# Sigmoid attention and mixture of depths: moving one pair's transposes and products between gaps of the attention steps

## The chip, the cores and the metric

The kernel runs on one core of a Trainium2 chip. Its time is device microseconds of one execution; before the change the median of 3 runs is 457.12 us (456.84 to 457.91). The profiled execution took 455.25 us, of which the profile shows a span of 453.4 us, at a mean granted TensorE clock of 0.996. All times within the execution are microseconds from the start of that span.

## The reference

```python
# attention: q, k, v are (8, 12, 448, 64), float32
scores = scale * q @ k^T - log(448)
attn   = 1 / (1 + exp(-scores))
x      = (attn @ v), heads joined -> (8, 448, 768)

# mixture of depths, w1 (768, 1024), w2 (1024, 768), capacity 128
for b in range(8):
    scores = x[b] @ w_gate
    top    = indices of the 128 largest scores
    xe     = x[b, top]
    h      = maximum(xe @ w1, 0)
    ye     = h @ w2
    out[b]      = x[b]
    out[b, top] = xe + sigmoid(scores[top])[:, None] * ye
```

All is float32. So a sequence's attention has to be complete before its 128 rows can be chosen, and only chosen rows go through the two matrices.

## The kernel before

**Steps and units.** Attention runs in 12 steps (`s` = 0 to 11). A step takes two groups of four heads, and three groups make a sequence, so a sequence is finished every one and a half steps. A step has 7 units (`n` = 0 to 6). `unit(s, n)` makes scores for both halves of the heads into two PSUM tiles `psc` (pool `ps_sc`, two buffers, so every unit uses both) with 32 recorded matmuls (L305), and ScalarE turns each tile into `attn_...` with one sigmoid of 128x896 (L313). After each unit comes `gap(s, n)`. Gaps 0 to 2 and 6 hold the products of the attention with `v` (`values`, L353): those of part 1 to 3 of step `s - 1` in gaps 0 to 2, part 0 of step `s` in gap 6. `take` (L368) turns the finished output into `x_b` in SBUF on VectorE.

**The choice of rows.** `gates` (L376, L379) multiplies `x_b` with the gate weights and sums, on VectorE; `gate` finishes the 448 scores of a sequence and writes them to DRAM (L404), `spread` reads them back broadcast over the partitions (`rep`, L416), `ranking` counts for each token how many are larger (L424, L427) and makes the selection mask `hot` (L439). `choose` is a small product of TensorE with the mask (L467, or L463 for some sequences), `fetch` turns its result into indices (L474, L477) and gathers the 128 rows `xe` from `out` (L488).

**The two matrices.** Sequences are taken in pairs `p`, so each product's weights are used for both. `turn_rows(b)`, written `("t", b)` in the table, transposes the rows of a sequence with six products with a unit matrix (L509); for the even sequence of a pair ScalarE copies the result to `rows_t` (L512), for the odd one ScalarE and VectorE copy half each (L514, L515), and VectorE makes three differences (L521) and, once product 2 has read its row, a last one (L531). Each of the two matrix products for a pair is done in the form with seven products of quarter matrices in place of eight, numbered 1 to 7. In the table `(m, p, key)` is product `key` of matrix `m` for pair `p`. `first` is 12 matmuls in the code, 24 records in the profile (L548), and its sums over `hidden` are on VectorE (L561) with rectifiers on ScalarE (L564, or the copy L567 for product 1); `second` is 4 in the code, 8 records (L613), and `second_sums` adds the result to `xe` on VectorE (L624), one operation for each quarter of `QUARTERS[key]`; the last one starts the scatter of the rows to `out` (L633). `hidden_sum` (L595, L599) makes four further sums of the hidden rows.

**What sets the order.** The schedule is written out by hand: each engine executes its instructions in the order in which the Python emits them, and waits are put in where one engine needs another. `WORK` says which transposes and products stand in gaps 3 to 5 of each step; they fill TensorE while ScalarE works on the sigmoids. Pairs 0 and 1 are done within the steps. Pair 2 (sequences 4 and 5) is begun in step 11 and done in `rest()`, the end part, followed by pair 3. In `rest()` the last sequence's scores, ranking and choice run on VectorE and the DMA queues while TensorE goes through pair 2.

**PSUM.** `banks(which)` hands out tiles of two banks: `psc` (two buffers) and two further ones, `o0` and `o1`. `"o"` alternates between these two, `"any"` alternates between `psc` and `o`. Within the steps, the transposes, products and `choose` take `"o"`, so a third user in a gap waits until the first one's tile has been read; `gap(s, 2)` sets the alternation back, so that the first in gap 3 has `o0`. `values(s, 0)` takes both.

**Weights.** Some quarter matrices stay in SBUF (`w1_sb`, `w2_sb`); the sums are kept in DRAM and lent (L208) into space of the attention: `LENT[11]` brings those of products 6, 7 and 5 of the first matrix into slots `d00` to `d02` as soon as step 10's attention output has been computed.

Of the kernel before, what the change touches and what calls it, by code (L numbers as in the profile page):

```python
# [17 lines left out]
def kernel(  # L18
# [475 lines left out]
    def bank(where):  # L494
        return banks(where)[:, 0]
# [42 lines left out]
    def first(p, key, where="o", ps=None):  # L538
        n = CAP
        x = pairs[p]["x"][:, ROWS1[key]]  # L540
        if key == 1:
            t = moe.tile([P, 7 * FH * P], F32, name="hidden")
            pairs[p]["h"] = t.rearrange("p (m k n) -> p m k n", m=7, k=FH)
        w = weight(1, key, p)
        ps = (bank(where) if ps is None else ps).rearrange("p (k n) -> p k n", n=P)
        for f in range(FH):
            for t in range(KH):
                nc.tensor.matmul(ps[:, f, :n], w((t * FH + f) * P, P), x[:, t, :n],  # L548
                                 start=(t == 0), stop=(t == KH - 1))
        if key == 2:  # L550
            pairs[p]["second"] = True
            last_row(p)
        return p, key, ps
# [77 lines left out]
    def scatter(b):  # L631
# [16 lines left out]
        (8, 3): [("t", 3), (1, 1, 1)], (8, 4): [(1, 1, 2), (1, 1, 6)],  # L648
        (8, 5): [(1, 1, 7), (1, 1, 4)],
        (9, 3): [(2, 1, 1), (2, 1, 2)], (9, 4): [(1, 1, 5)], (9, 5): [(1, 1, 3), (2, 1, 4)],  # L650
        (10, 3): [(2, 1, 3)], (10, 4): [(2, 1, 5), (2, 1, 6)], (10, 5): [(2, 1, 7)],
        (11, 3): [("t", 4)], (11, 4): [("t", 5), (1, 2, 1)], (11, 5): [(1, 2, 2)],
    }

    LENT = {5: [(1, 6), (1, 7), (1, 5)], 6: [(1, 3), (2, 4), (2, 5)], 7: [(2, 6), (2, 7)],
# [3 lines left out]
    def begin(item, where="o"):  # L659

        m, p, key = item
        return (first if m == 1 else second)(p, key, where)
# [87 lines left out]
    def rest():  # L750
# [4 lines left out]
        p, b = NP - 2, B - 1  # L755
        for key, slot in (((2, 6), "d10"), ((2, 7), "d11")):
            lend(*key, slot)
        shared = banks("any")
        chosen = choose(b - 1, shared[:, 1])
        work = [((1, p, 6), first(p, 6, ps=shared[:, 0])),  # L760
                ((1, p, 7), begin((1, p, 7), "any"))]
        gates(2 * NS - 1)
        fetch(*chosen)

# [3 lines left out]
        store(b, (2, 3))  # L768
        for item, args in work:
            finish(item, args)  # L770
        for key in (4, 5):
            do((1, p, key), "any")
        first_sums(*begin((1, p, 3), "any"), sums_too=(5, 6))
        work = {key: begin((2, p, key), "any") for key in (2, 1, 4)}
        ranking(b)
        tile5 = banks("any")
        work[5] = second(p, 5, ps=tile5[:, 0])
        chosen = choose(b, tile5[:, 1])
        second_sums(*work[2])
        hidden_sum(p, 7)  # L780
        work[6] = begin((2, p, 6), "any")
        fetch(*chosen)
        second_sums(*work[1])
        hidden_sum(p, 3)
        work[7] = begin((2, p, 7), "any")
        for key in (4, 5, 6, 7):
# [95 lines left out]
```

## Time and profile before

| engine | busy, us | share of the span |
|---|---|---|
| TensorE (PE) | 442.0 | 97% |
| TensorE weight loads (PEld) | 267.0 | 59% |
| VectorE (DVE) | 303.8 | 67% |
| ScalarE (ACT) | 181.8 | 40% |
| GpSimd (POOL) | 32.5 | 7% |

Busy shares of these engines by stage, and what the DMA engines did:

| window, us | what runs | PE | DVE | ACT | DMA share | GB/s |
|---|---|---|---|---|---|---|
| 320 to 340 | end of step 10 | 20.00 | 11.12 | 7.79 | 0.53 | 147 |
| 340 to 360 | step 11 | 19.41 | 11.37 | 11.38 | 0.65 | 164 |
| 360 to 380 | step 11, start of the end part | 18.84 | 11.61 | 3.28 | 0.95 | 211 |
| 380 to 400 | pair 2 | 20.00 | 18.45 | 1.23 | 0.77 | 171 |
| 400 to 420 | pair 2, pair 3 | 20.00 | 11.88 | 2.71 | 0.18 | 60 |
| 420 to 440 | pair 3 | 20.00 | 11.94 | 1.26 | 0.00 | 1 |

A row of a timeline has the start, the length, the engine, the line, the operation, its output and inputs, its shape, and the count of instructions merged into it; in brackets stands how long the engine was idle before it and whose work ended the wait. Matmuls overlap, so the length of a merged row is somewhat longer than the distance to the next row's start. A row also counts as busy while a later instruction in it waits.

### The profile page before, as it was taken

Reading aid. Unit: us, or ns where it says so; the run is one execution under the profiler, and the core shown is the slowest. Engines: PE = TensorE matmul, PEld = TensorE weight load, DVE = VectorE, ACT = ScalarE, POOL = GpSimd, SP = SyncE. Lnnn points to the kernel's source line nnn. Section 1 sums busy time; section 2 is a strip of 40 time slices with the busy share of each in tenths; the row PEclk is TensorE's granted clock in tenths of the full one; section 3 lists DMA queues with packets and bytes.
Section 4 is the critical chain, followed back from the end, with each engine's and each line's share of the span. In section 5 each row is a group of like instructions: output and inputs, shape, how many; then the busy total and the mean of one; then the engine's idle time right before and its main releaser. Section 6 shows DMA issues by size and latency. Waiting matters only on the chain.

```text
span 453.4 us, 14452 instructions
## 1 busy us (share of the span) xinstructions
PE 442.0 (97%) x6398; PEld 267.0 (59%) x6398; DVE 303.8 (67%) x663; ACT 181.8 (40%) x237; POOL 32.5 (7%) x55
## 2 busy tenths in 40 slices
PE   8999999999999999999999999999999989999994
PEld 3474745565745845554445855654454639769952
DVE  4308679993844797887634697897742849994472
ACT  3856464555555254335444345334345520101100
POOL 7000000010000100000100000010010000001001
PEclk9999999999999999999999999999999999999998
DMA  8898898999866995995566883994833999811001
GB/s 279 214 329 193 329 342 187 267 205 319 175 201 220 139 234 192 170 233 186 117 235 174 132 222 142 193 196 159 241 106 101 259 189 267 147 37 71 1 0 69
DMA packets 128334, 84.67 MB, mean 187 GB/s; under 512 B 97600, under 2 KB 112064, under 8 KB 128272
## 3 DMA queue, kind: packets, MB, share of 16 engines
q1 hardware_dynamic: 126288, 75.84, 65.1%
q0 software_dynamic: 1984, 7.91, 5.7%
q8 instruction: 50, 0.82, 0.8%
q14 instruction: 12, 0.10, 0.1%
HBM read 63.28 MB, written 20.46 MB: 185 GB/s over the span
## 4 chain that ended last, share of the span: by engine, by line
PE 93%; DVE 3%; issue 1%; ACT 1%; DMA 1%; POOLq 0%; DVEq 0%; ACTq 0%
PE o L353 28%; PE psc L305 27%; PE o L548 13%; PE o L613 12%; PE psc L548 4%; PE psc L613 3%; PE o L305 3%; PE o L818 1%; PE o L326 1%; DVE x_b L368 1%; DMA out_dram<-xe,idx 1%; ACT attn_u L313 1%; DVE gate_p L379 1%; DVE scr L376 1%; PE o L467 0%
## 5 line engine op out<-in xcount | busy, mean ns | idle before, releaser
L305 PE MATMUL psc<-qT,kT 32*64 32x448 f32 x2496 | 148.2, 540 | 0.9 <-ACT attn_u L313 0.9
L313 ACT ACTIVATE attn_u<-psc,bias_s 128x896 f32<-128x896 f32 x86 | 81.9, 1004 | 84.4 <-PE psc L305 84.3
L353 PE MATMUL o<-attn_d,raw_v 32*64 32x448 f32 x960 | 104.5, 535 | 0.4 <-ACT o L356 0.4
L353 PE MATMUL o<-attn_u,raw_v 32*64 32x448 f32 x960 | 102.2, 535 | 0.8 <-ACT o L356 0.8
L305 PEld LDWEIGHTS psc<-qT,kT 32*64 32x64 f32 x2496 | 60.2, 131 | 59.1 <-issue 40.3
L313 ACT ACTIVATE attn_d<-psc,bias_s 128x896 f32<-128x896 f32 x70 | 66.7, 1003 | 46.5 <-PE psc L305 46.4
L368 DVE STREAM_TRANSPOSE x_b<-o 128x448 f32<-128x448 f32 x48 | 26.9, 618 | 66.6 <-PE o L353 59.3
L353 PEld LDWEIGHTS o<-attn_u,raw_v 32*64 32x64 f32 x960 | 41.2, 132 | 24.9 <-issue 19.9
L353 PEld LDWEIGHTS o<-attn_d,raw_v 32*64 32x64 f32 x960 | 40.4, 132 | 19.9 <-issue 17.3
L548 PEld LDWEIGHTS o<-rows_t,w_sb 128*128 128x128 f32 x264 | 30.4, 192 | 4.5 <-issue 1.4
L548 PEld LDWEIGHTS o<-rows_t,attn_d 128*128 128x128 f32 x264 | 30.3, 192 | 3.9 <-DVE scr L376 1.4
L548 PE MATMUL o<-rows_t,w_sb 128*128 128x128 f32 x264 | 31.9, 278 | 0.4 <-DVE rows_t L515 0.3
L548 PE MATMUL o<-rows_t,attn_d 128*128 128x128 f32 x264 | 31.6, 277 | 0.3 <-DVE rows_t L521 0.3
L379 DVE TENSOR_REDUCE gate_p<-scr 128x14 f32<-128x448 f32 x48 | 29.8, 622 | 1.7
L376 DVE TENSOR_TENSOR scr<-x_b,wg_b 128x448 f32<-128x448 f32 x48 | 29.6, 616 | 1.0
L624 DVE SCALAR_TENSOR_TENSOR xe<-o,gate,xe 128x384 f32<-128x384 f32 x37 | 21.1, 611 | 13.4 <-PE o L613 13.3
L280 DVE STREAM_TRANSPOSE kT<-raw_k 128x384 f32<-128x384 f32 x46 | 23.5, 548 | 6.9 <-PE psc L305 3.6
L613 PE MATMUL o<-attn_d,hidden 128*128 128x384 f32 x80 | 27.7, 494 | 0.0
L564 ACT ACTIVATE hidden<-hidden 128x512 f32<-128x512 f32 x12 | 7.5, 630 | 48.1 <-DVE hidden L561 48.1
L424 DVE TENSOR_SCALAR_CACHE_REDUCE scr<-rep,who 128x448 f32<-128x448 f32 (+1 forms) x32 | 21.5, 671 | 7.2 <-DMA rep<-scores 6.2
L613 PE MATMUL o<-w_sb,hidden 128*128 128x384 f32 x72 | 24.7, 491 | 0.0
L561 DVE TENSOR_TENSOR hidden<-o,hidden 128x512 f32<-128x512 f32 x24 | 16.0, 686 | 12.0 <-PE o L548 11.8
(117 smaller groups left out, 478.3 us busy)
## 6 DMA issues: line engine op xcount, KB each, us to landing
attn_d<-sum SPq DMA_DIRECT2D x42, 384.0 KB
out_dram<-x_b SPq DMA_DIRECT2D x32, 336.0 KB
raw_k<-in_k_dram SPq DMA_DIRECT2D x23, 448.0 KB
raw_q<-in_q_dram SPq DMA_DIRECT2D x23, 448.0 KB
raw_v<-in_v_dram SPq DMA_DIRECT2D x40, 192.0 KB
w_sb<-in_moe_w_dram SPq DMA_DIRECT2D x6, 768.0 KB
sum<-hidden SPq DMA_DIRECT2D x6, 768.0 KB
rep<-scores POOLq DMA_DIRECT2D x7, 224.0 KB, 5.3
```

The lines of the kernel that those rows point to most:

```text
L280: nc.vector.transpose(kT[i][:, e, :HK], sk[:, e, :HK].rearrange("p (m c) d -> p c m d", c=NF))
L305: nc.tensor.matmul(psc[h // 2][y * Dh:(y + 1) * Dh, h % 2, :S], kT[2 * s + x][d, e, r:r + 2, :].rearrange("d r t -> d (r t)"), qT[2 * s + ...
L313: nc.scalar.activation(a, psc[pr][:, :, :S], AF.Sigmoid, bias=bias_s, scale=QK_SCALE)
L353: nc.tensor.matmul(o[x][j * Dh:(j + 1) * Dh, pr, :S], w, a[rows, j, :], start=(n == 0 and c == 0), stop=(n == 3 and c == NF - 1))
L368: nc.vector.transpose(x_tiles[b][:, :, 2 * g + pr, :], outs[s][x][:, pr, :S].rearrange("p (r t) -> p r t", t=TT))
L376: nc.vector.tensor_tensor(out=tmp, in0=x_tiles[b][:, :, hp, :], in1=wg_b[:, hp:hp + 1, :].to_broadcast([P, TB, TT]), op=ALU.mult)
L379: nc.vector.tensor_reduce(out=gate_parts[b][:, :, hp], in_=tmp, axis=AX.X, op=ALU.add)
L424: nc.vector.tensor_scalar(out=junk[:n], in0=rep[:n], scalar1=own, scalar2=0.0, op0=ALU.is_gt, op1=ALU.add, accum_out=above[:n, c:c + 1])
L548: nc.tensor.matmul(ps[:, f, :n], w((t * FH + f) * P, P), x[:, t, :n], start=(t == 0), stop=(t == KH - 1))
L561: nc.vector.tensor_tensor(out=dst, in0=a, in1=b, op=ALU.add)
L613: nc.tensor.matmul(ps[:n, :DH], h[:, t, :n], w(t * DH, DH), start=(t == 0), stop=(t == FH - 1))
L624: nc.vector.scalar_tensor_tensor(out=xe[:n, cols], in0=ps[:n, :DH], scalar=st[b]["gate"][:n, 0:1], in1=xe[:n, cols], op0=ALU.mult, op1=ALU ...
```

## The change

Three edits belong together.

- In the table, the transposes of sequence 4 move from gap 3 of step 11 to the end of gap 5 of step 10. The three gaps of step 11 are filled anew: product 1 of pair 2 in gap 3, the transposes of sequence 5 and product 2 in gap 4, product 6 in gap 5. Before, they held the transposes of sequence 4; those of sequence 5 and product 1; product 2. So every gap is to have a product, and one product more of pair 2 is done within step 11.
- In `rest()`, product 6 is therefore gone from the end part. Products 7 and 4 of the first matrix are now those that are issued ahead of the last gate work, then 5 and 3.
- Of the second matrix, products 1 and 2 change places, both where they are issued and where their sums are taken.

```diff
-        (10, 3): [(2, 1, 3)], (10, 4): [(2, 1, 5), (2, 1, 6)], (10, 5): [(2, 1, 7)],
-        (11, 3): [("t", 4)], (11, 4): [("t", 5), (1, 2, 1)], (11, 5): [(1, 2, 2)],
+        (10, 3): [(2, 1, 3)], (10, 4): [(2, 1, 5), (2, 1, 6)], (10, 5): [(2, 1, 7), ("t", 4)],
+        (11, 3): [(1, 2, 1)], (11, 4): [("t", 5), (1, 2, 2)], (11, 5): [(1, 2, 6)],
...
-        work = [((1, p, 6), first(p, 6, ps=shared[:, 0])),
-                ((1, p, 7), begin((1, p, 7), "any"))]
+        work = [((1, p, 7), first(p, 7, ps=shared[:, 0])),
+                ((1, p, 4), begin((1, p, 4), "any"))]
...
-        for key in (4, 5):
-            do((1, p, key), "any")
+        do((1, p, 5), "any")
         first_sums(*begin((1, p, 3), "any"), sums_too=(5, 6))
-        work = {key: begin((2, p, key), "any") for key in (2, 1, 4)}
+        work = {key: begin((2, p, key), "any") for key in (1, 2, 4)}
         ranking(b)
         tile5 = banks("any")
         work[5] = second(p, 5, ps=tile5[:, 0])
         chosen = choose(b, tile5[:, 1])
-        second_sums(*work[2])
+        second_sums(*work[1])
         hidden_sum(p, 7)
         work[6] = begin((2, p, 6), "any")
         fetch(*chosen)
-        second_sums(*work[1])
+        second_sums(*work[2])
         hidden_sum(p, 3)
```

The number and the kind of the instructions of every engine stay as they were; only their order and the banks of some products differ.

## The prediction

> **What bounds the kernel now.** I read the page's busy table first, then the chain of waits, then TensorE's own timeline where the change falls, then VectorE's and ScalarE's beside it. Steps are named as in the code: (11, 3) is the gap after unit 3 of step 11.
>
> ```profile
> PE 442.0 (97%) x6398; PEld 267.0 (59%) x6398; DVE 303.8 (67%) x663; ACT 181.8 (40%) x237; POOL 32.5 (7%) x55
> PE 93%; DVE 3%; issue 1%; ACT 1%; DMA 1%; POOLq 0%; DVEq 0%; ACTq 0%
> ```
>
> TensorE is the bound, with 11 us of its 453.4 us span without work, and 7% of the chain lies on other engines. The edit keeps every product, so it can pay only by closing idle time of TensorE, and it costs whatever idle it opens. A "busy" matmul row also stretches over a wait in its middle, so I compare start times. TensorE at the end of step 10 and in step 11:
>
> ```profile
> 327.97 2.85 PE L613 MATMUL o<-attn_d,hidden 128*128 128x384 f32 x8
> 330.65 0.50 PE L463 MATMUL o<-ones,sums 128*128 128x1 f32 x4
> 331.08 1.76 PE L305 MATMUL psc<-qT,kT 32*64 32x448 f32 x32
> ...
> 349.37 0.85 PE L509 MATMUL o<-iden,xe 128*128 128x128 f32 x6
> 350.55 2.65 PE L305 MATMUL psc<-qT,kT 32*64 32x448 f32 x32 [0.33 <-ACT attn_u L313]
> 353.12 0.87 PE L509 MATMUL o<-iden,xe 128*128 128x128 f32 x6
> ...
> 358.63 2.94 PE L548 MATMUL o<-rows_t,w_sb 128*128 128x128 f32 x24 [0.26 <-DVE rows_t L515]
> ```
>
> An unhindered unit takes 1.70 us from start to next start, a set of turned rows (six transposes) 0.7, a product 2.7 (first matrix) or 2.6 (second). After the first six transposes of step 11, unit 4 should begin at 350.03 and be over at 351.72. It is over at 353.12: the 0.7 us of work in gap 3 is too short to cover ScalarE emptying the score banks of unit 3 (two sigmoids, 349.48 to 351.39). Lost: 1.40 us. The rest of gaps 3 to 5 holds another 0.68 us, half of it the 0.26 wait in the last line. So step 11 offers about 2.08 us.
>
> In the end part TensorE runs without a gap from 375.65, the selection product of sequence 6 (this moment is T below), to its last matmul. But VectorE is barely ahead there:
>
> ```profile
> 392.94 0.68 DVE L424 TENSOR_SCALAR_CACHE_REDUCE scr<-rep,who 128x448 f32<-128x448 f32 x1 [0.37 <-DMA rep<-scores]
> ...
> 398.93 0.69 DVE L439 TENSOR_TENSOR hot<-slots,place_s 128x512 f32<-128x512 f32 x1
> 399.54 0.61 DVE L624 SCALAR_TENSOR_TENSOR xe<-o,gate,xe 128x384 f32<-128x384 f32 x1
> ```
>
> Sequence 7's selection mask `hot` is ready at 399.62, T + 23.97. TensorE asks for it at 400.37, T + 24.72. Slack 0.75 us, and the ranking ahead of it began when the broadcast of the scores landed. That is a chain of fixed length from T (attention output, gates, scores out, scores back, ranking), and TensorE's work beside it is what the edit shortens.
>
> [...] the 0.26 us wait of a product on L515 lies behind 0.62 us gate operations on VectorE that have nothing to do with it. [...] I use that as the lower bound for the scores' write, which took from 386.03 (end of its issue) to 389.93, when the read back could be issued: 3.9 us.
>
> **The change part by part.** All times are on the clock of before.
>
> 1. *Turned rows of sequence 4 at the end of step 10.* No product is added, the 0.7 us moves. But `choose(5)` comes behind it in the same gap, and it takes the next accumulator bank, now the one of product (2, 1, 7), whose two L624 sums (1.14 us) start only when that product ends. Before, `choose(5)` got the other bank. The same sequence of instructions stands at the end of step 7: product (2, 0, 7), turned rows of sequence 2, `choose(3)`:
>
> ```profile
> 221.18 2.85 PE L613 MATMUL o<-attn_d,hidden 128*128 128x384 f32 x8
> 223.86 0.82 PE L509 MATMUL o<-iden,xe 128*128 128x128 f32 x6
> 225.26 0.61 PE L463 MATMUL o<-ones,sums 128*128 128x1 f32 x4 [0.58 <-DVE xe L624]
> 225.80 1.76 PE L305 MATMUL psc<-qT,kT 32*64 32x448 f32 x32
> ```
>
> From product to unit: 4.62 us there, 331.08 - 327.97 = 3.11 at step 10. So everything after moves by **D = 1.51 us**, 0.7 of it the moved work and 0.8 new wait. ScalarE's copy (0.81) and the later fetch of sequence 5 lie beside unit 6 and attention products. Bounds 0.66 (no wait) to 1.51.
>
> 2. *A product in each gap of step 11.* Product 1 in gap 3 covers the sigmoids (2.7 against the 2.0 needed), so the 1.40 us is gone. Subtracting D: product 1 at 349.37, unit 4 at 352.15, turned rows of 5 at 353.84, product 2 at 354.55, unit 5 at 357.3, product 6 from 359.0. Product 6 reads row group 5, which VectorE makes last but one in L521. VectorE's queue there is continuous from the L368 transposes at 348.09 and depends on the attention output alone, so it moves by D and no more: L515 at 358.02, L521 three times 0.53 from 358.49, so row 5 at about 359.6. Product 6 waits 0.6 us and is over at 362.4.
>
>    The larger wait is ScalarE's. Before, product 2 stood in gap 5, and its rectifier (L564, which waits for VectorE's L561) was queued behind the sigmoids of unit 5. Now product 2 stands in gap 4, so L564 is queued **ahead of unit 5's sigmoids**. VectorE reaches that L561 behind L521 and L531: 360.1 + 0.5 (L531) + 0.7 = 361.24. Then L564 (0.63, next start 0.54 later) lets the sigmoids start at 361.82. Until they are done, unit 6 has no score banks. In the sample of unit 3 and 4 above, from the sigmoids' start (349.48) to the operation after the next unit (353.12) took 3.64. So the attention products after unit 6 begin at 361.82 + 3.64 = 365.46, and on the clock of before at 363.06. Step 11 with one product more is thus 2.40 us longer, and T moves by 1.51 + 2.40 = **3.91 us**. Lower bound, if the rectifier held nothing: unit 6 at 362.4, T moves by 1.51 + 1.04 = 2.55. The weights of product 6 are no question: they are lent first, at 346.54, and raw_h issues that wait for these lanes pass by 358.7.
>
> 3. *End part with one product less ahead of the selection.* Relative to T: `choose(6)` 0.91, four products 10.72, so 11.63; (2, 1) takes the bank of product 7, freed by its two L561 after the gate chain of sequence 7 (386.17 - T = 10.52, plus 1.29), so it starts at 11.86; four products of the second matrix 10.33: TensorE reaches `choose(7)` at 22.19. The mask, unchanged, is ready at 23.97: 1.8 us wait. Next, (2, 6) takes the bank of (2, 1), and because (2, 1) and (2, 2) have changed places all four L624 sums of (2, 1) (2.18 us in the row of before, there after the selection) stand between `hot` and that bank; `choose(7)` itself takes 0.8 of it. So (2, 6) begins at 23.97 + 2.18 = 26.15, against 401.18 - T = 25.53 before: **+0.62**. The one product less, 2.68 us, has bought nothing.
>
>    Upper end of what may come back: the lends into `kT` and `qT` (0.79 MB, issued 373.2 to 376.4) don't wait for T, so with T 2.4 us later against them they are off the DMA engines earlier. At the 332 GB/s of the window 380 to 382 this is 2.4 us of queue. [...] the ranking begins when VectorE is free, at about T + 16.2 (six L561 and two L595/L599, where before it had seven: 16.9), not T + 17.3. That gives 1.1 us back, so the end part is -0.48. I take -0.3, near this end, since all that backlog is issued before T.
>
>    Behind that point the order is the same but for the swapped banks, and fetch 7 has room: before, its rows landed some 4 us after 402.28 and were used at 412.33.
>
> Sum: 1.51 + 2.40 - 0.3 = **+3.6 us**, 460.7 us; 4.5 with a fixed scores chain.
>
> **Rivals.**
> - *The gaps fill as meant*: 2.08 us of step 11 come back, only product 6's wait and the step-10 wait (0.6 + 0.8) are paid, and the end part hides its chain: -0.7 to -1.2, about 456.1. For it: product 1 does cover the sigmoids. Against it: 24.7 us of TensorE work cover 24.0 us of chain now, and 22.2 cannot.
> - *The rectifier does not hold the sigmoids* (VectorE's chain ahead of L561 shorter than I add up): T moves by 2.55, end part +0.6 at most: about 460.0.
> - *The end part loses nothing*, the scores landing much sooner: 3.91 - 2.68 = +1.2, 458.3. Against it: VectorE's 6.7 us of ranking cannot start before its sums are through.
>
> **How the numbers follow.** My forecast (460.2 to 461.7) gets 0.67, the second rival 0.10, the third 0.09, the first 0.11, and 0.03 for no change by cancelling. The range 458.8 to 461.9 reaches over the second rival and leaves out the first, most of the third, and the tails. Faster 0.11, same 0.03, slower 0.86.
>
> **What would show it.** In the profile after: L463 behind six transposes at the end of step 10 with a wait of about 0.6 us on L624; unit 4 of step 11 with no wait; an L564 on ScalarE between the sigmoids of units 4 and 5 with some 4 us of idle before it, and unit 6 waiting on ScalarE; the selection product L467 of sequence 7 waiting on VectorE, and (2, 6) behind it waiting on L624. I am wrong if ScalarE has its sigmoids of unit 5 on time, or if `hot` comes before T + 22.2.

## The result and the profile after

The change makes the kernel slower, and by somewhat more than forecast. The first measurement gave 463.04 us (median of 4 executions, 462.65 to 463.29) against 457.51 (4, 456.84 to 458.10) of the kernel before: ratio 1.0121 [1.0103, 1.0139]. The forecast was 460.7, with a range up to 461.9. The same kernel measured three more times, each time beside the kernel before, gave 1.0074 [1.0049, 1.0098], 1.0081 [1.0052, 1.0111] and 1.0091 [1.0059, 1.0123], or +3.2, +3.9 and +3.7 us by the medians: close to the +3.6 of the forecast. The first set of four was thus an unlucky one. Three of its four executions have a mean clock of 0.993 to 0.995, which in every execution profiled here went with TensorE's clock at half for some microseconds ahead of the last matmul; the fourth, the profiled one, kept its clock but was late before the change begins. Executions more than 1.5% above the fastest of their kernel (three of the kernel before, one of choose_shares below) are left out of the ratios, though not of the medians and counts.

The two lines of the page after, busy times and the engine shares of the chain that ended last:

```profile
PE 446.8 (97%) x6398; PEld 278.5 (60%) x6398; DVE 303.4 (66%) x663; ACT 182.0 (39%) x237; POOL 33.1 (7%) x55
PE 83%; DVE 10%; DMA 3%; issue 2%; ACT 1%; POOLq 0%; DVEq 0%; ACTq 0%
```

The counts are the same; in the chain, 10 points have gone from TensorE, most of them to VectorE and the DMA engines. Only part of that is the change. In the end part the chain leaves TensorE from 395.92 to 408.82 for VectorE's sums, the ranking and the mask of sequence 7. The other detour, from 70 to 91 us over the scores and the ranking of sequence 0 (all the DMA time but the last 3 us), lies in a part that no edit touched.

I cut both traces at five points: **A**, the first sum (L624) of product (2, 1, 7), which is the last thing before the first moved instruction; **X**, the first transpose (L368) of step 10's output; **T** and **C**, the selection products of sequences 6 and 7; **R**, the first transpose (L509) of sequence 6's rows in the end part. All lengths are us; "before, 2nd" is a second profile of the kernel before (before_again below).

| profile | A | A to X | X to T | T to C | C to R | R to end | A to end |
|---|---|---|---|---|---|---|---|
| before | 330.86 | 17.23 | 27.56 | 24.72 | 6.05 | 46.94 | 122.50 |
| before, 2nd | 331.83 | 17.94 | 27.55 | 24.72 | 6.05 | 46.95 | 123.22 |
| after | 335.61 | 18.74 | 29.64 | 22.77 | 7.37 | 46.94 | 125.46 |
| after less before | +4.75 | +1.51 | +2.08 | -1.95 | +1.32 | 0.00 | +2.96 |

The profiled execution of after is 7.7 us longer than that of before, and 4.75 of it lie ahead of A, where both programs are the same. The price in this pair of traces is 2.96 us. Against the second profile of before, in which the attention products of step 10 took 0.7 us longer, it is 2.24. TensorE's timeline of after, end of step 10:

```profile
332.73 2.85 PE L613 MATMUL o<-attn_d,hidden 128*128 128x384 f32 x8
335.41 0.82 PE L509 MATMUL o<-iden,xe 128*128 128x128 f32 x6
336.81 0.61 PE L463 MATMUL o<-ones,sums 128*128 128x1 f32 x4 [0.58 <-DVE xe L624]
337.35 1.76 PE L305 MATMUL psc<-qT,kT 32*64 32x448 f32 x32
```

It is step 7's sequence over again: 4.62 us from product to unit, the selection product waiting 0.58 us for the sums of the product whose bank it takes. ScalarE's timeline in step 11, before:

```profile
358.44 1.91 ACT L313 ACTIVATE attn_u<-psc,bias_s 128x896 f32<-128x896 f32 x2 [1.13 <-PE psc L305]
362.80 0.63 ACT L564 ACTIVATE hidden<-hidden 128x512 f32<-128x512 f32 x1 [2.46 <-DVE hidden L561]
```

and after:

```profile
360.36 1.90 ACT L313 ACTIVATE attn_u<-psc,bias_s 128x896 f32<-128x896 f32 x2 [1.13 <-PE psc L305]
...
367.45 0.63 ACT L564 ACTIVATE hidden<-hidden 128x512 f32<-128x512 f32 x1 [4.72 <-DVE hidden L561]
367.99 1.89 ACT L313 ACTIVATE attn_u<-psc,bias_s 128x896 f32<-128x896 f32 x2
```

Before, the rectifier of product 2 (L564) comes behind the sigmoids of unit 5 (L313, the row at 358.44). After, it waits 4.72 us at the head of ScalarE's queue for VectorE's sum, and these sigmoids begin only behind it, at 367.99. And the end part, TensorE:

```profile
406.77 1.05 PE L467 MATMUL o<-who,hot 128*128 128x2 f32 x8 [0.25 <-DVE hot L439]
408.87 2.85 PE L613 MATMUL psc<-attn_d,hidden 128*128 128x384 f32 x8 [1.05 <-DVE xe L624]
411.55 2.74 PE L613 MATMUL o<-attn_d,hidden 128*128 128x384 f32 x8
```

The selection product waits for the mask, and product (2, 6) behind it waits 1.05 us for the four sums of (2, 1) that read the bank it takes. Between 406.51, when the row ahead of these ends, and 408.87 TensorE has one product of 2 columns and nothing else. Such a stretch without a product wider than 2 columns is called a hole below; this one is 2.4 us long.

### The profile page after: what moved, and what is told of

Read it like the earlier page. It is cut to its first block, busy times and chain, and to the rows that moved or that the text cites. A ratio compares the mean times of both kernels' runs of the same rounds, so it can differ in the third digit from the quotient of the medians.

```text
span 461.1 us, 14457 instructions
## 1 busy us (share of the span) xinstructions
PE 446.8 (97%) x6398; PEld 278.5 (60%) x6398; DVE 303.4 (66%) x663; ACT 182.0 (39%) x237; POOL 33.1 (7%) x55
## 4 chain that ended last, share of the span: by engine, by line
PE 83%; DVE 10%; DMA 3%; issue 2%; ACT 1%; POOLq 0%; DVEq 0%; ACTq 0%
PE o L353 26%; PE psc L305 24%; PE o L548 12%; PE o L613 10%; PE psc L548 4%; PE psc L613 2%; PE o L305 2%; DMA scores<-total 2%; DVE x_b L368 2%; DVE scr L427 1%; PE o L817 1%; DVE scr L424 1%; DVE xe L624 1%; ACT attn_u L313 1%; DVE gate_p L379 1%
## 5 line engine op out<-in xcount | busy, mean ns | idle before, releaser
L305 PE MATMUL psc<-qT,kT 32*64 32x448 f32 x2496 | 154.4, 541 | 1.0 <-ACT attn_u L313 0.6
L313 ACT ACTIVATE attn_u<-psc,bias_s 128x896 f32<-128x896 f32 x86 | 82.0, 1004 | 86.0 <-PE psc L305 85.9
L353 PE MATMUL o<-attn_d,raw_v 32*64 32x448 f32 x960 | 108.3, 535 | 0.7 <-issue 0.4
L353 PE MATMUL o<-attn_u,raw_v 32*64 32x448 f32 x960 | 106.0, 535 | 0.8 <-ACT o L356 0.8
L305 PEld LDWEIGHTS psc<-qT,kT 32*64 32x64 f32 x2496 | 65.5, 132 | 57.4 <-issue 36.3
L313 ACT ACTIVATE attn_d<-psc,bias_s 128x896 f32<-128x896 f32 x70 | 66.7, 1004 | 46.9 <-PE psc L305 46.8
L368 DVE STREAM_TRANSPOSE x_b<-o 128x448 f32<-128x448 f32 x48 | 26.9, 616 | 75.2 <-PE o L353 67.8
L353 PEld LDWEIGHTS o<-attn_d,raw_v 32*64 32x64 f32 x960 | 46.1, 132 | 18.8 <-issue 14.4
L353 PEld LDWEIGHTS o<-attn_u,raw_v 32*64 32x64 f32 x960 | 44.1, 132 | 21.9 <-issue 15.7
L624 DVE SCALAR_TENSOR_TENSOR xe<-o,gate,xe 128x384 f32<-128x384 f32 x36 | 20.5, 611 | 13.3 <-PE o L613 13.3
L548 PEld LDWEIGHTS o<-rows_t,w_sb 128*128 128x128 f32 x216 | 24.8, 192 | 3.9 <-issue 1.4
L564 ACT ACTIVATE hidden<-hidden 128x512 f32<-128x512 f32 x12 | 7.5, 631 | 49.6 <-DVE hidden L561 49.6
L548 PE MATMUL o<-rows_t,w_sb 128*128 128x128 f32 x216 | 26.2, 278 | 0.1
L561 DVE TENSOR_TENSOR hidden<-o,hidden 128x512 f32<-128x512 f32 x25 | 16.7, 686 | 12.8 <-PE o L548 12.5
```

The source lines that it names most:

```text
L305: nc.tensor.matmul(psc[h // 2][y * Dh:(y + 1) * Dh, h % 2, :S], kT[2 * s + x][d, e, r:r + 2, :].rearrange("d r t -> d (r t)"), qT[2 * s + ...
L313: nc.scalar.activation(a, psc[pr][:, :, :S], AF.Sigmoid, bias=bias_s, scale=QK_SCALE)
L353: nc.tensor.matmul(o[x][j * Dh:(j + 1) * Dh, pr, :S], w, a[rows, j, :], start=(n == 0 and c == 0), stop=(n == 3 and c == NF - 1))
L368: nc.vector.transpose(x_tiles[b][:, :, 2 * g + pr, :], outs[s][x][:, pr, :S].rearrange("p (r t) -> p r t", t=TT))
L561: nc.vector.tensor_tensor(out=dst, in0=a, in1=b, op=ALU.add)
L624: nc.vector.scalar_tensor_tensor(out=xe[:n, cols], in0=ps[:n, :DH], scalar=st[b]["gate"][:n, 0:1], in1=xe[:n, cols], op0=ALU.mult, op1=ALU ...
```

## The experiments

Two questions: where the 2 to 3 us come from (a bank wait in step 10, a queue wait in step 11, the hole in the end part), and why the first time lies above the sum. All ratios are to the kernel before, measured in the same set.

### How much of the difference is chance: the two kernels again

No edit. First the kernel before against itself:

> The kernel before, unchanged, run and profiled once more. In the profiles on record the changed kernel is already 4.76 us late when unit 5 of step 10 starts on TensorE (331.04 against 326.28), ahead of every instruction that the change moves; 3.5 us of it arise before step 2, in waits of TensorE called issue. Theory S (the drift is chance of an execution, and the profile of before was a lucky one): step 2 begins anywhere between 49 and 53 us in this run, and the time is 456.8 to 458.1. Theory P (the drift belongs to the program): step 2 begins at 49.1 us within 0.5 us, as in the profile of before.

458.57 us (456.42 to 460.58, 12 executions) against 458.47: ratio 0.9997 [0.9974, 1.0021]. Then the changed kernel, three times:

> The changed kernel, unchanged, run and profiled once more. Theory S: step 2 begins anywhere between 49 and 53 us. Theory P: at 52.6 us within 0.5 us. In both, what the change does from step 10 on is the same as in its profile: 1.5 us at the end of step 10, 2.1 us in step 11, 0.6 us back in the end part, 2.95 us in all beyond the drift.

461.63 us (460.29 to 464.52, 11), ratio 1.0074 [1.0049, 1.0098].

> The changed kernel unchanged, beside the two that follow on the same chip, so that they can be compared under one set of runs. 3 to 4.5 us slower than the kernel before. From the end of product (2, 1, 7) to the end of the execution 125.5 us if the clock stays at 1.00 in the end part, 127.2 with one window of 3.4 us at 0.50, up to 129 with two; the kernel before takes 122.5 to 123.2.

460.90 us (459.59 to 463.41, 6), ratio 1.0081 [1.0052, 1.0111].

> The changed kernel once more, beside the kernel with seven dummies. Both theories: 460.9 to 463 us, about two executions in three at a mean clock of 0.995 or less.

462.44 us (460.15 to 465.42, 8), ratio 1.0091 [1.0059, 1.0123].

The 4.75 us ahead of A did not come back: A lay at 333.77, 332.42 and 332.60 in these three profiles, and at 331.83 in the second one of before. The first sigmoid of step 2 alone spread from 48.82 (after_fourth) and 49.08 (before) over 49.73 and 50.24 to 52.62 us (the first after). So a profile's early part tells nothing of this change. What did come back was a second difference. In after_again the end part reads:

```profile
405.78 1.05 PE L467 MATMUL o<-who,hot 128*128 128x2 f32 x8 [1.12 <-DVE hot L439]
407.88 4.54 PE L613 MATMUL psc<-attn_d,hidden 128*128 128x384 f32 x8 [1.05 <-DVE xe L624]
412.26 2.75 PE L613 MATMUL o<-attn_d,hidden 128*128 128x384 f32 x8
```

The same product (2, 6), same shape, takes 4.54 us instead of 2.85, and waits for nothing in its middle. The windows of this profile (busy time of PE, PEld, DVE, ACT and POOL, then the granted TensorE clock, the DMA share and GB/s) say why:

```profile
405.00:408.00 3.00, 1.17 (x9) 1.09 (x10) 2.96 (x6) 0.00 (x0) 0.00 (x0) 1.00 0.01 3
408.00:412.00 4.00, 4.00 (x8) 2.19 (x9) 3.26 (x8) 0.00 (x0) 1.29 (x1) 0.57 0.18 29
412.00:415.00 3.00, 3.00 (x12) 1.76 (x11) 1.67 (x3) 0.00 (x0) 0.00 (x0) 1.00 0.23 92
```

Behind the hole, where PE was busy for 1.17 of 3 us, the clock drops to a half. Read slice by slice it is at 0.50 from 408.58 for 3.41 us, and then at 1.00 again. In after_third it was at 0.50 for 6.83 us from 405.42, twice 3.41, and C to R took 10.41 instead of 7.37. After_fourth, like the first profile of after, kept 1.00 and 7.37. The price of one stretch in after_again, where C to R took 9.06, is 9.06 - 7.37 = 1.7 us, half its length; of the two in after_third it is 3.0, since part of them fell into the hole itself.

The hole ahead of it, with the thin (2-column) selection product in it, was 3.2 us long in after_again and 2.8 in after_third; in after and after_fourth, where the clock held, it was 2.4. What decides is worked out below, after the experiments on the hole.

Every timed execution lists its mean clock. Sorted at 0.995 or less against 0.996 or more (one stretch lowers the mean by 3.41 x 0.5 / 460 = 0.0037; the mean also counts stretches elsewhere, behind the last matmul too, so it sorts roughly; in the 17 profiles of this case it puts the 8 that have such a stretch ahead of the last matmul apart from the 9 that have none), with the median time of each class:

| kernel | executions | 0.996 or more | their time | 0.995 or less | their time |
|---|---|---|---|---|---|
| before, all sets | 156 | 122 (78%) | 457.26 | 34 (22%) | 459.68 |
| after, all sets | 29 | 9 (31%) | 460.29 | 20 (69%) | 462.98 |

The table pools sets whose levels differ (the kernel before had medians of 457.0 to 458.8). Compared within a set, the change costs 2.2 to 2.8 us in the class of the full clock and 2.4 to 3.7 in the other, from 2 to 8 executions of the changed kernel each. Besides, it moves 47% of the executions into the class that is 2 to 3 us longer: an estimated 1.2 us in the mean. Of the four executions of the first measurement three were in it.

### The rectifier behind the sigmoids

```diff
-        (11, 4): [("t", 5), (1, 2, 2)], (11, 5): [(1, 2, 6)],
+        (11, 4): [("t", 5), ("b", 1, 2, 2)], (11, 5): [("f", 1, 2, 2), (1, 2, 6)],
...
```

`"b"` issues the product, `"f"` its sum (L561) and rectifier (L564), now behind unit 5's sigmoids.

> The changed kernel with one edit: the sum and the rectifier of product 2 are emitted in gap 5 of step 11, behind the sigmoids of unit 5, and not in gap 4 ahead of them. TensorE's order is the same. My theory (the rectifier holds the sigmoids, these the score banks of unit 6): the sigmoids of unit 5 start some 1.5 us or more earlier, unit 6 waits no more for ScalarE, and the end part begins 1.0 to 1.4 us earlier, counted from unit 5 of step 10. The rival (unit 6 is held by product 6's wait for its row group or by something else): no shift. In the end the gain is 1.0 us less what the scores chain of the end part gives back, so 0.3 to 1.3 us faster than the changed kernel.

ScalarE's timeline has the two changed round, with no wait ahead of the rectifier:

```profile
361.33 1.91 ACT L313 ACTIVATE attn_u<-psc,bias_s 128x896 f32<-128x896 f32 x2 [2.79 <-PE psc L305]
363.26 0.63 ACT L564 ACTIVATE hidden<-hidden 128x512 f32<-128x512 f32 x1
```

X to T fell from 29.65 to 28.66, so the rectifier did hold the sigmoids, and through them the step, for 1.0 us. The time did not follow, against the 0.3 to 1.3 us expected: 462.52 us (458.98 to 463.56, 7), ratio 1.0076 [1.0037, 1.0114]. T came 1.0 earlier, but T to C grew from 23.63 (after_again) to 24.39, and the clock was at 0.50 for 6.83 us behind it.

### The gate work after product 6

The other way to free the queue: VectorE's gate work (`gates` of sequence 7's earlier part) stands in gap 3 ahead of what the rectifier waits for; it is moved into gap 5.

```diff
-            gates(2 * s - 1)
+            if s < NS - 1:
+                gates(2 * s - 1)
...
+        if (s, n) == (NS - 1, 5):
+            gates(2 * s - 1)
```

> The changed kernel with one edit in step 11: the gate operations of head group 21 (four of VectorE, 2.6 us) are emitted behind product 6 in gap 5, and not ahead of the transposes of sequence 5. My theory (the differences of rows, the sum and the rectifier of product 2 come late because VectorE's queue is full, and through them the sigmoids of unit 5 and the banks of unit 6): both waits go, and from the first transposition of step 10's output to T it takes 27.4 to 27.9 us, where the changed kernel takes 29.64 and the one with the later rectifier 28.66. Rival (ScalarE or the banks are the limit by themselves): 28.6 or more. The time falls by less than the 2 us, since the end part then waits longer for the mask and its clock may fall for longer: 0 to 2 us faster than the changed kernel.

X to T fell by 1.6, to 28.06, somewhat short of what was expected: 0.5 us longer than before for a step that has one product (2.7 us) more. The time again did not follow: 462.18 us (459.25 to 463.78, 12), ratio 1.0089 [1.0063, 1.0114]. T to C grew to 24.45, a 3.41 us stretch at half clock began at 407.27, and 11 of the 12 executions had a clock of 0.995 or less.

These two show why T is not what counts. In after, after_again, relu_later and gates_later the read of sequence 7's scores was issued at T + 12.50, 13.81, 14.37 and 14.53, latest after T in the two where T came early; from A to C it took 71.15, 72.02, 71.79 and 71.24. T moves by up to 1.6 us against A, and C by no more than the two profiles of the changed kernel differ. What varies is the write of the scores: from the end of its issue until the read back could be issued it took 2.13, 3.45, 4.10 and 4.16 us. So with an earlier T the ranking waits for the scores to land (1.6 us on VectorE in each of the two kernels).

### The selection of sequence 5 in the product's own tile

```diff
-        (10, 5): [(2, 1, 7), ("t", 4)],
+        (10, 5): [("c", 5, (2, 1, 7)), ("t", 4)],
...
+            tile = banks(where)
+            args = second(*item[2][1:], ps=tile[:, 0])
+            chosen = choose(item[1], tile[:, 1])
+            second_sums(*args)
+            fetch(*chosen)
...
```

A tile has two banks and the product uses one; `choose(5)` takes the other, ahead of the transposes, and waits for no sum.

> The changed kernel with one edit: at the end of step 10 the selection product of sequence 5 goes into the second bank of the tile of product (2, 1, 7), and stands ahead of the transposes of sequence 4, so that it needs no third accumulator tile. My theory (it waited for the two sums of that product): the wait of 0.58 us ahead of it goes, and unit 6 of step 10 starts 0.85 us earlier counted from unit 5; all of step 11 and the end part keep it: 0.8 us faster than the changed kernel. The rival (the transposes themselves cost 1.5 us there): no more than 0.2 us faster.

TensorE at the end of step 10:

```profile
330.40 2.85 PE L613 MATMUL o<-attn_d,hidden 128*128 128x384 f32 x8
333.08 0.50 PE L463 MATMUL o<-ones,sums 128*128 128x1 f32 x4
333.45 0.85 PE L509 MATMUL o<-iden,xe 128*128 128x128 f32 x6
334.23 1.76 PE L305 MATMUL psc<-qT,kT 32*64 32x448 f32 x32
```

3.83 us from product to unit instead of 4.62, no wait: A to X falls by 0.76, to 17.98. The time stays at 462.59 us (460.08 to 467.94, 10), ratio 1.0067 [1.0040, 1.0093], with 7 of 10 executions at the lower clock. The gain is in the trace, locally, and not in the time.

### Products 1 and 2 in their old order

The changed kernel without its third edit (swap_back, below), and that edit alone put into the kernel before (swap_only, the same lines the other way round):

```diff
-        work = {key: begin((2, p, key), "any") for key in (1, 2, 4)}
+        work = {key: begin((2, p, key), "any") for key in (2, 1, 4)}
...
-        second_sums(*work[1])
+        second_sums(*work[2])
...
-        second_sums(*work[2])
+        second_sums(*work[1])
```

> The changed kernel with products 1 and 2 of the second matrix in their former order again, in issue and in sums; the step table stays changed. My theory (behind the mask, product 6 waits 1.05 us for the four sums of product 1 in its bank): the wait behind the selection product goes, since one sum (0.6 us) fits beside it; TensorE may lose up to 1.3 us ahead of the mask on the rectified row of product 2, which the wait for the mask hides. From the selection product of sequence 7 to the turned rows of sequence 6 then 6.0 to 6.2 us at full clock, where the changed kernel takes 7.37. The clock may still fall, since the mask is waited for as before. 0.5 to 1.5 us faster than the changed kernel. Rival (the exchange is free): 7.3 us or more and no gain.

```profile
394.74 2.85 PE L613 MATMUL psc<-w_sb,hidden 128*128 128x384 f32 x8 [1.45 <-ACT hidden L564]
...
405.17 0.95 PE L467 MATMUL o<-who,hot 128*128 128x2 f32 x8
405.98 2.83 PE L613 MATMUL psc<-attn_d,hidden 128*128 128x384 f32 x8
```

The hole behind the selection product is gone: product (2, 6) follows 0.81 us after it. So is the wait ahead of it, because product (2, 2), now first, waits 1.45 us for its rectifier ten microseconds earlier. All 20 executions had a clock of 0.996 or more. 459.46 us (458.39 to 460.63), ratio 1.0041 [1.0024, 1.0059]: about half of the loss is undone. C to R is 6.05, as expected, but T to C is 23.75, so from T to R the gain on the profile of after is only 0.3 us (29.80 against 30.14). The larger part of what is undone is thus the clock, which no longer falls: among the executions with the full clock this kernel is still 2.8 us slower than the kernel before of its set (459.46 against 456.66).

> The kernel before with the third edit alone: products 1 and 2 of the second matrix exchanged, in issue and in sums. TensorE reaches the last selection product when the mask is ready, as before, so the only wait is that of product 6 for the four sums of product 1 in its bank, behind the mask: from T to the turned rows of sequence 6 31.3 to 31.6 us, where before takes 30.77; clock 1.00 throughout, since the hole is under 1 us of wait. 0.4 to 0.8 us slower than before. Rival (the exchange is free when product 6 of the first matrix is still in the end part): 30.8 us, and no difference.

458.03 us (455.76 to 462.52, 20), ratio 1.0030 [1.0013, 1.0048], with 15 of 20 at the full clock; C to R was 6.27 against 6.05. Less than I expected in the trace, where (2, 6) waited only 0.2 us for the sums. So the exchange costs 1.3 us from C to R in the changed kernel and 0.2 here. The 1.0 us by the medians is more than these 0.2; another 0.7 of the profile lie from X to T (28.23), where nothing was edited, and their cause is not shown.

### Does the hole stop the clock?

Wide dummy products (128x192, read by nobody; the kernel before has the same in steps 1 to 3, L326) in the changed kernel, first only in the wait ahead of the selection product:

```diff
+        for _ in range(4):
+            nc.tensor.matmul(tile5[:, 1, P:P + HP * TT], iden,
+                             wg_b.rearrange("p h t -> p (h t)"), start=True, stop=True)
         chosen = choose(b, tile5[:, 1])
```

> The changed kernel with four idle products of TensorE (unit matrix times gate weights, 0.33 us each, results unused) ahead of the selection product of sequence 7 in the end part, where TensorE waits 0.6 to 2.0 us for VectorE's mask anyway. In three of four profiles of changed kernels the granted clock fell to 0.50 for 3.4 or 6.8 us right behind that wait, and products 6 and 7 of the second matrix took up to twice their time; in the fourth, with the shortest wait, it did not. Theory G (the hole in the end part trips the clock): with the hole filled the clock stays at 1.00 through the end part, from T to the turned rows of sequence 6 TensorE takes 30.0 to 31.3 us where these profiles show 30.1, 32.3, 32.7 and 34.7, and the median falls by 0.5 to 2 us against the changed kernel. Rival (the clock falls by chance of the execution): still 0.50 in this stretch, no gain or a loss of up to 1 us.

461.57 us (459.28 to 463.55, 7), ratio 1.0091 [1.0052, 1.0129]; a second time:

> The changed kernel with four idle products ahead of the last selection product, a second time, since the 7 times of its first run scattered over 4.3 us. Theory G (the hole in the end part trips the clock): no window at 0.50 in the end part, and a median 0.5 to 2 us under that of the changed kernel in this set. Rival (the clock falls by chance): a window at 0.50 in the profile, or the same median within 0.3 us.

461.44 us (458.76 to 464.72, 6), ratio 1.0104 [1.0067, 1.0140]. Neither profile has a half clock ahead of the last matmul, and 9 of 13 executions are at 0.996 or more, but the medians did not fall. By the time this was a miss; by the clock it was not settled. So the second half of the hole was filled too, with three more such products right behind the selection product:

> The changed kernel with seven dummy products of 128x192 (nothing reads them): four ahead of the selection product of sequence 7, three right behind it, in the bank of that product. The reference's outputs are kept. Clock theory: with both waits filled by full-width products, the only thin work left is the selection product itself (0.8 us), so no 3.41 us window at half clock in the end part and at most 1 execution in 5 at a mean clock of 0.995 or less (the changed kernel: 2 in 3); the time is then 460.0 to 460.8 with the dummies' own length beyond the waits (at most 0.5 us) in it, against 461 to 463 of the changed kernel. Rival, that the half clock has nothing to do with the hole: the share stays at 1 in 2 or more and the time does not fall below the changed kernel's by more than 0.3.

```profile
404.83 1.46 PE L778 MATMUL o<-wg_b,iden 128*128 128x192 f32 x8
406.64 1.05 PE L467 MATMUL o<-who,hot 128*128 128x2 f32 x8 [0.34 <-DVE hot L439]
407.55 1.22 PE L782 MATMUL o<-wg_b,iden 128*128 128x192 f32 x6
408.74 2.85 PE L613 MATMUL psc<-attn_d,hidden 128*128 128x384 f32 x8
```

9 of 10 executions had the full clock, against 2 of 8 of the changed kernel beside it. The time was 461.75 us (459.61 to 463.07, 10), ratio 1.0059 [1.0034, 1.0083], against 462.44 and 1.0091 [1.0059, 1.0123]; the intervals overlap, and the absolute figure missed the expected 460.0 to 460.8 in a set where the kernel before, too, took 458.75. So the share of the clock came out as expected; the gain in time, 0.7 us, is not resolved. At the full clock alone the kernels with dummies are no faster than the changed kernel of their set (459.86 against 459.60 for the second with four, 461.51 against 460.85 for the one with seven), so what filling gains in clock they may lose by their own length; the executions are too few to say.

The converse, in the kernel before: no idling, but thin work, to see whether that keeps the clock up. Twelve products of 2 columns ahead of the selection product:

```diff
+        for _ in range(12):
+            nc.tensor.matmul(tile5[:, 1, P:P + 2], iden,
+                             wg_b.rearrange("p h t -> p (h t)")[:, :2], start=True, stop=True)
         chosen = choose(b, tile5[:, 1])
```

> The kernel before with twelve dummy products of 2 columns (24 records of some 0.1 us, 2.4 us, nothing reads them) right ahead of the selection product of sequence 7. The reference's outputs are kept. TensorE then never idles, but does thin work for some 3.2 us on end. Theory [...]: half or more of the executions at a mean clock of 0.995 or less (before: 2 in 9), a 3.41 us window at half clock behind the selection product in the profile, and 459 to 461.5 us. Rival, that any matmul in the queue keeps the clock: 2 in 9 as before, no such window, and 2.4 us longer than before at most (459.4).

TensorE's timeline, then the windows:

```profile
401.42 2.74 PE L779 MATMUL psc<-wg_b,iden 128*128 128x2 f32 x24
404.01 1.38 PE L467 MATMUL psc<-who,hot 128*128 128x2 f32 x8
405.25 5.47 PE L613 MATMUL o<-attn_d,hidden 128*128 128x384 f32 x8
```

```profile
402.00:405.00 3.00, 3.00 (x27) 3.00 (x27) 0.03 (x1) 0.00 (x0) 0.00 (x0) 0.92 0.00 0
405.00:409.00 4.00, 4.00 (x8) 2.42 (x9) 3.57 (x9) 0.00 (x0) 1.00 (x1) 0.50 0.20 40
```

PE counts as busy for every microsecond of it, with 27 matmuls in 3 us, and yet the clock goes to 0.50, for 6.8 us, so that a product of 2.85 takes 5.47. All 6 executions were at 0.995 or less. 463.95 us (462.36 to 467.82), ratio 1.0127 [1.0085, 1.0169]: longer than I expected, since there were two stretches and not one. The rival, that any matmul in the queue keeps the clock up, has fallen.

The traces also show why one execution is hit and the next is not. In all 17 profiles the clock changes only at whole multiples of 3.413 us, counted from the first entry of the clock record, which lies 4.5 to 7.6 us into the span, differently in each execution (before: at 5.70, and the first change, behind the last matmul, 130 multiples later at 449.43; after: at 7.54, and 132 later at 458.10; in after_again two falls lie 15 apart, in tiny 16). Cut the span by this grid, and count in each window the time without a product wider than 2 columns. Ahead of the last matmul the clock falls from 1.00 to 0.50 ten times, and each time the window just ended had 1.97 to 3.21 us of such time. No window after which the clock stayed at 1.00 had more than 1.98. So in these profiles about 2.0 us of the 3.41 decide, and the hole of the end part counts only as far as it falls into one window:

| profile | hole | largest part of it in one window, us | then |
|---|---|---|---|
| after | 406.52 to 408.87 | 1.98 | 1.00 |
| after_fourth | 403.50 to 405.86 | 1.53 | 1.00 |
| after_third | 403.33 to 406.08 | 2.08 | 0.50, two windows |
| after_again | 404.66 to 407.88 | 2.72 | 0.50, one window |

Here are the windows of after and of after_again; the selection product is 0.92 and 1.05 us of their PE time:

```profile
406.90:410.31 3.41, 2.36 (x13) 1.74 (x14) 3.41 (x9) 0.00 (x0) 0.06 (x1) 1.00 0.01 2
405.17:408.58 3.41, 1.75 (x10) 1.46 (x11) 3.41 (x9) 0.00 (x0) 0.00 (x0) 1.00 0.01 2
```

The 0.50 lasted a second window in the three profiles (after_third, relu_later, tiny) in which the first half-clock window itself still had 0.67 to 0.86 us of the hole, and ended after one where it had none.

### Two attempts at a better kernel

The first joins gates_later and choose_shares, and in the end part takes the sums of (2, 2) and product 7's hidden sum ahead of the ranking, and issues (2, 6) ahead of the selection product.

```diff
+        second_sums(*work[2])
+        hidden_sum(p, 7)
         ranking(b)
...
+        work[6] = begin((2, p, 6), "o")
         chosen = choose(b, tile5[:, 1])
...
```

> The changed kernel with four edits: the gate operations of head group 21 behind product 6; the selection product of sequence 5 in the second bank of product (2, 1, 7)'s tile; the sums of product 2 of the second matrix and the hidden sum of product 7 ahead of the last ranking; product 6 of the second matrix ahead of the last selection product, in the bank that product 2 has left. By my account: step 10 as before plus 0.8 us, step 11 as before or 0.1 more with one product more in it, from T to the turned rows of sequence 6 28.9 us, where before takes 30.8, and the clock at 1.00. In all 1.0 us less than the kernel before, 0.5 to 1.5. Rival (the end part is set by VectorE's chain whatever TensorE does beside it): 30.8 us or more there, and 0.8 us slower than before.

A miss: 459.09 us (456.09 to 461.89, 22), ratio 1.0042 [1.0021, 1.0064]. The sum put ahead of the ranking waits 1.27 us on VectorE for its own product, and with it everything behind it, so the mask came at T + 25.2. The selection product waited for it (0.16), the next product 1.05 for the indices, and 15 of 22 executions had the lower clock. From T to R it took 31.73 us, as the rival has it.

The second keeps the two joined edits, splits what sequence 7's gate needs only for itself (`own_scores`) off from the path to DRAM, finishes product 4 and the sums in the order in which their readers come, and puts one product ahead of the selection and one behind it into banks that are free by then:

```diff
-        work = {key: begin((2, p, key), "any") for key in (1, 2, 4)}
+        work = {key: begin((2, p, key), "any") for key in (2, 1, 4)}
+        own_scores(b)
         second_sums(*work[2])
         hidden_sum(p, 7)
         ranking(b)
...
+        work[6] = begin((2, p, 6), "psc")
         chosen = choose(b, tile5[:, 1])
+        second_sums(*work[4])
+        work[7] = begin((2, p, 7), "psc")
         second_sums(*work[1])
...
```

> The changed kernel with the edits of the two that helped (gate operations of head group 21 behind product 6; the selection product of sequence 5 in the second bank of product (2, 1, 7)'s tile) and an end part without a hole: the sums that free the rectified row of product 2 come first and the copies of sequence 7's own scores later; products 2, 1, 4, 5 and then 6 of the second matrix stand ahead of the last selection product, and product 7 takes the bank of product 4, which needs one sum, not four. By my account from T to the turned rows of sequence 6 28.0 to 28.6 us (before 30.77), step 11 28.05 (before 27.56), step 10 0.4 to 0.8 more than before, clock at 1.00: 1.3 to 2.3 us faster than the kernel before. Rival (VectorE's chain sets the end part whatever stands beside it): 29.5 us or more there, and no gain.

```profile
406.10 2.74 PE L617 MATMUL psc<-attn_d,hidden 128*128 128x384 f32 x8
408.68 0.95 PE L471 MATMUL o<-who,hot 128*128 128x2 f32 x8
409.49 2.83 PE L617 MATMUL psc<-attn_d,hidden 128*128 128x384 f32 x8
```

No wait on either side of the selection product, and 28.11 us from T to R, as expected. 456.04 us (454.51 to 461.18, 23), ratio 0.9973 [0.9956, 0.9989]: faster than the kernel before by 1.0 us, with the extra product in step 11 kept. That is less than the 1.3 to 2.3 us expected. A to end is 120.72 against 122.50, and 18 of 23 executions had the full clock.

## Why the prediction was partly right

The direction was right, and so were the three places in which the change costs time; the time of the first measurement, 463.04 us, lies above the range, which ended at 461.9.

- **What bounds the kernel.** Right. The edit paid only with idle time of TensorE, and the trace has it where the prediction looked for it.
- **Turned rows at the end of step 10**, 1.51 predicted. From product to unit it is 4.62 against 3.11, to the hundredth, and of that 0.76 was undone when the selection took the product's own tile. That A to X also gives 1.51 is luck of the pair: against the second profile of before it is 0.80.
- **Step 11**, +2.40 predicted, +2.08 measured. Unit 4 waits no more. The sigmoids of unit 5 start at 367.99, which on the prediction's clock (less 4.75 and 1.51) is 361.73, where it has 361.82; so the 0.3 us too many lie behind them, in the 3.64 us taken from the sample of units 3 and 4. That the rectifier at the head of ScalarE's queue holds them is shown by moving it (-1.0) and by bringing its input earlier (-1.6). The rival in which it holds nothing has fallen, and so has the one in which the gaps fill as meant.
- **The end part.** That the mask decides, that (2, 6) waits behind it for four sums, and that some of the DMA backlog comes back: all seen. From T to R, 30.3 to 31.4 was predicted, -0.3 against before taken; 30.14 was measured where the clock held, -0.63. The write of the scores took 2.13 us there, against 3.9 before (386.03 to 389.93); the lower bound that the prediction sets under it was not shown by any trace. The ranking began at T + 16.04 without a wait, where it has T + 16.2. In after_again the write took 3.45. The third rival, in which the end part loses nothing, has fallen: -2.68 would have been needed.
- **The step that failed** is the end of part 3: "Behind that point the order is the same but for the swapped banks". It lets everything behind the selection product run at its old length once the wait is over, and so puts at nothing what the wait does to the clock. The wait itself was priced (1.8 us for the mask, of which 0.25 to 1.1 came, and the sums' bank). What the runs showed in place of that nothing: with the hole of 2.4 to 3.2 us the clock fell to 0.50 in two of four profiles of the changed kernel, T to R was then 32.69 and 33.58, +1.9 and +2.8 against before, and 20 of 29 executions have the lower mean clock, against 22% of the kernel before.
- **What of this is luck.** At the full clock the forecast of +3.6 stands against 2.2 to 3.0 measured. The clock adds an estimated 1.2 in the mean, so that the three later sets, at +3.2 to +3.9, lie around the forecast: local costs somewhat too high and a clock left out cancel there. In the first set three of four executions had the lower clock and the fourth had lost 4.75 us before A; that put it above the range. The three were not profiled, so that their half clock stood in the end part is inferred from the other sets.
- The base was slightly too smooth as well: the profile of before (455.25) is faster than any of the three times given with it, and 22% of the executions of the kernel before have a lowered clock somewhere.

What stays open: why half-filling the hole lowered the share of slowed clocks and not the median, which 13 executions do not resolve; and the lowered clocks of the kernel before. Three profiles (gates_later, best, best2) have a 3.41 us stretch at half clock from 89.8 to 91.7 us on, in a part that no edit touched. It follows the selection product of sequence 0, which has waits beside it: the window ahead had 1.97, 2.43 and 3.04 us without a product wider than 2 columns. In the two profiles of before the largest such window there has 1.44 and 1.1 us, and their clock held. The same hole, falling otherwise on the grid, would account for the lowered clocks of before; no execution of it that had one was profiled.

## What to carry to other kernels

Filling a gap of the bounding engine did not pay here while it put something in the queue of a partner ahead of what the next step needed: product 2 left a rectifier that waited 4.72 us ahead of the sigmoids, and moving it took 1.0 us off X to T. So look at what the moved piece leaves for the other engines, and in which queue. Where another engine's chain (scores to DRAM, back, ranking, mask) ran beside the work that was shortened, the saved time became a wait: with X to T shorter by 1.0 and by 1.6 us, VectorE waited 1.6 for the scores. And a wait on TensorE had two prices, its length (1.05 us for the sums in front of (2, 6)) and the clock afterwards (1.7 us for one stretch in after_again): keep wide products on both sides of a thin one, as the last kernel does, so that the hole stays well under the 2.0 us at which the clock fell here.

## What was not expected of the hardware

- Ahead of the last matmul TensorE's clock fell to 0.50, for 3.41 or 6.83 us, ten times in 17 profiles, each time right behind a window of 3.41 us that had 1.97 us or more without a product wider than 2 columns; no window with less was followed by a fall. The windows lie differently in each execution, so the same hole of 2.4 to 3.2 us catches some executions of one program and not others; about 7 of 10 had the lower mean clock. One stretch cost 1.7 us (after_again).
- In 20 of 20 executions the mean clock stayed at 0.996 or more where the selection product had wide products on both sides and the longest single wait of the end part was 1.45 us (swap_back).
- Matmuls of 2 columns counted as busy in the profile but did not keep the clock up: over 32 records on end, 3.8 us, it went to 0.50 for 6.8, and all 6 executions had a mean of 0.987 to 0.994 (tiny).
- The early part of this kernel scatters by several us with no edit: A lay between 330.86 and 335.61 in six profiles of the two programs, before and after.
